# Attention scores as two 64-row products beside each other instead of one 128-row product against a key tile padded with zeros

## The chip, the cores and the metric

One core of one Trainium2 chip runs the whole program in one launch. The metric is the time of one execution in device microseconds. The kernel before took 731.09 us, the median of three runs (729.94 to 734.69).

## The reference, cut to what matters

Three stages follow each other. The attention has 8 batches, 8 heads, 576 tokens and a head width of 64; keys and values are averaged over groups of 8 tokens, which leaves 72 keys per head. A soft mixture of experts and a two-layer network come behind it.

```python
k_p = k.reshape(B, H, Sp, pool, D).mean(axis=3)            # pool 8, Sp 72
scores = scale * np.matmul(q, k_p.transpose(0, 1, 3, 2))   # (8, 8, 576, 72)
scores = scores - np.max(scores, axis=-1, keepdims=True)
attn = np.exp(scores)
attn = attn / (np.sum(attn, axis=-1, keepdims=True) + 1e-09)
attn_out = np.matmul(attn, v_p)
# then: soft mixture of experts (8 experts, 32 slots), then
h = x @ w_in; r = np.maximum(h, 0.0); g = s * (r * r) + b; out = g @ w_out
```

All of it is float32. The softmax over 72 keys is taken for each of 8 x 8 x 576 rows.

## The kernel before, in words

The first third of the program is the attention with the dispatch of its rows to the expert slots. Batches are taken in pairs (`pr` = 0 to 3), and each pair is cut into nine units of 128 token rows by some heads: unit 0 is mixed (the last 64 tokens of both batches, all heads two at a time), units 1 to 8 are pure (one batch). There are 36 units: 4 mixed and 32 pure. A pure unit takes four heads, and for each of them two token rows `t` that lie beside each other in memory: 2 x 64 numbers fill the 128 partitions of a transposed query tile.

A unit passes through six stages, named by letters, which a hand-written table (`LOOP`, `FIRST` and `TAIL`) orders so that stages of up to six units alternate on the engines' queues. Stage A (`st_A`) transposes the queries on TensorE, and ScalarE copies them into `qT` (L355). Stage B (`st_B`) makes the scores of the unit in two banks of `sc` and lets VectorE take the maximum `mx` (L390) and subtract it into `S` (L393). Stage C (`st_C`) is the exponential on ScalarE (L397), the sum and its reciprocal on VectorE (L401 to L404) and the product with it on GpSimd into `P` (L421). Stages D, E and F transpose `P` back (L434, L435), multiply it with the values that were folded with the slot matrix (L457, L464), and transpose that (L480). Between them stand the steps of `dispatch` for a finished batch (L545 to L611) and of `prep` for the next pair's keys and values (`kv_transpose`: L264 on TensorE, then copies by ScalarE, L273 for keys and L285 for values).

The pooled keys stand in `kb_t[pr % 2]`, one tile for even and one for odd pairs: 128 partitions, 16 heads of the pair, 2 x 72 columns. Partitions 0 to 63 and 64 to 127 hold the same keys, the first at columns 0 to 71 and the second at columns 72 to 143; the rest is zero, set once at the start by GpSimd (L231). So one product of 128 rows by 144 columns gives the 72 scores of both token rows (L383), four such products a unit. A mixed unit makes 16 products of 64 rows, 64 weight columns and 72 columns instead (L376), on the four quarters of the array in turn. A float32 product stands as two records in the trace, each with its own weight load, so a pure unit has eight records and a mixed one 32. Transposes by the identity have one record each.

When the attention is over, the experts' weights run over TensorE (L933, L941) while their loads still land, and the two-layer network (L1010, L1067) takes the rest.

Of the kernel before, what the change touches and what calls it, by code (L numbers as in the profile page):

```python
# [10 lines left out]
F32 = mybir.dt.float32  # L11
# [45 lines left out]
def kernel(  # L57
# [14 lines left out]
    nc = tc.nc  # L72
    B, H, SEQ, D = q.shape
    KP = SEQ // 8
# [133 lines left out]
    sc2 = sctx.enter_context(tc.tile_pool(name="sc2", bufs=2, side="right"))  # L208
    apb = bctx.enter_context(tc.tile_pool(name="apb", bufs=1, side="right"))
    P2_all = [p.tile([128, 2, H, KP], F32, name=f"P2_{i}") for i, p in enumerate((apc, apc, ap1, ap1, apb, apb))]  # L210
    pp1 = pctx.enter_context(tc.tile_pool(name="pp1", bufs=1, side="right"))
# [3 lines left out]
    def bank():  # L215
        return ps_w.tile([128, 512], F32, tag="w", name="w")
# [9 lines left out]
    make_identity(nc, ident)  # L226
    nc.vector.memset(one, 1.0)
    phi_t = pp1.tile([128, 4, 32], F32, name="phi_t")
    kb_t = [p.tile([128, 2 * H, 2 * KP], F32, name=f"kb{i}", bufs=1) for i, p in enumerate((pp1, sc2))]
    for i in range(2):  # L230
        nc.gpsimd.memset(kb_t[i], 0.0)  # L231
    for i in range(NPR):
        nc.gpsimd.memset(L_t[i], -3.0e38)

# [24 lines left out]
    def kv_transpose(nm, pr, c):  # L259

        src = kvp[nm, pr]
        ps = bank()
        for i in range(3):
            nc.tensor.transpose(  # L264
                out=ps[:, 128 * i:128 * i + 128],
                in_=src[:, 3 * c + i].rearrange("p t d -> p (t d)"),
                identity=ident,
            )
        if nm == "k":
            for h2 in range(2):  # L270
                r = slice(64 * h2, 64 * h2 + 64)
                o = kb_t[pr % 2][r, :, KP * h2 + 24 * c:KP * h2 + 24 * c + 24]
                nc.scalar.activation(  # L273
                    out=o.rearrange("p n (g u) -> p g n u", g=3),
                    in_=ps[r, 0:384].rearrange("p (g n u) -> p g n u", g=3, u=8),
                    func=ACTF.Copy, scale=1.0 / 64,
                )
            return
        if pr not in vt_t:
            vt_t[pr] = pp1.tile([128, 2, 4, KP], F32, tag="vt", name="vt", bufs=1)  # L280
        for h2 in range(2):
            r = slice(64 * h2, 64 * h2 + 64)
            o = vt_t[pr][r].rearrange("p b c x -> p (b c) x")[:, :, 24 * c:24 * c + 24]
            i_ = ps[r, 0:384].rearrange("p (g n t u) -> p g n t u", g=3, n=8, t=2)[:, :, :, h2, :]
            nc.scalar.activation(out=o.rearrange("p n (g u) -> p g n u", g=3), in_=i_, func=ACTF.Copy, scale=1.0 / 8)  # L285
# [47 lines left out]
    qT_t, S_t, P_t, P2_t, PT_t, LT_t = {}, {}, {}, {}, {}, {}  # L333
    SLOT = [5, 1, 2, 3, 4, 6, 7, 8, 9]

    def parts(jj):
        if jj == 0:
            return [(0, slice(0, 64)), (1, slice(64, 128))]
        return [(0 if jj < 5 else 1, slice(0, 128))]
# [25 lines left out]
    def st_B(t):  # L365
        pr, u = divmod(t, 9)
        qT = qT_t.pop(t)
        kb = kb_t[pr % 2]
        sc = ps_s.tile([128, 2, 512], F32, tag="sc", name="sc")
        if u == 0:  # L370

            for i in range(4):
                for x in range(2):
                    p = slice(64 * x, 64 * x + 64)
                    for bb, r in parts(0):
                        nc.tensor.matmul(  # L376
                            out=sc[r, x, KP * i:KP * i + KP], lhsT=qT[p, i, r],
                            rhs=kb[p, H * bb + 2 * i + x, KP * x:KP * x + KP], start=True, stop=True,
                        )
        else:  # L380
            bb, j = divmod(u - 1, 4)
            for i in range(4):
                nc.tensor.matmul(  # L383
                    out=sc[:, i // 2, 2 * KP * (i % 2):2 * KP * (i % 2) + 2 * KP],
                    lhsT=qT[:, i, :], rhs=kb[:, H * bb + 4 * (j % 2) + i, :], start=True, stop=True,
                )

        scv = sc[:, :, 0:288].rearrange("p x (i k) -> p x i k", k=KP)
        mx = ap2.tile([128, 2, 4], F32, tag="mx", name="mx")
        nc.vector.tensor_reduce(out=mx, in_=scv, axis=AX.X, op=ALU.max)  # L390
        S = sc2.tile([128, 2, 4, KP], F32, tag="S", name="S", bufs=2)
        S_t[t] = S
        nc.vector.tensor_tensor(out=S, in0=scv, in1=mx.unsqueeze(3).to_broadcast([128, 2, 4, KP]), op=ALU.subtract)  # L393

    def st_C(t):
        S = S_t[t]
        nc.scalar.activation(out=S, in_=S, func=ACTF.Exp)  # L397
        pr, u = divmod(t, 9)
        S = S_t.pop(t).rearrange("p x i k -> p (x i) k")
        sm = ap2.tile([128, 8], F32, tag="sm", name="sm")  # L400
        nc.vector.tensor_reduce(out=sm, in_=S, axis=AX.X, op=ALU.add)  # L401
        nc.vector.tensor_scalar(out=sm, in0=sm, scalar1=1e-9, scalar2=None, op0=ALU.add)
        rs = ap2.tile([128, 8], F32, tag="rs", name="rs")
        nc.vector.reciprocal(out=rs, in_=sm)  # L404
        rb = rs.unsqueeze(2).to_broadcast([128, 8, KP])
        if u == 0:
            P = (ap1 if pr % 2 else apb).tile([128, H, KP], F32, tag="Pm", name="Pm")
            P_t[t] = P
            o = P.rearrange("p (i x) k -> p x i k", x=2)
            S, rb = (z.rearrange("p (x i) k -> p x i k", x=2) for z in (S, rb))  # L410
        else:
            j = (u - 1) % 4
            if j % 2 == 0:
                n = 4 * pr + (u - 1) // 2
                P2 = P2_all[n % 6 if pr < NPR - 1 else n % 4]
                P2_t[0] = P2
                P_t[t], P_t[t + 1] = P2[:, 0], P2[:, 1]
            h0 = 4 * (j % 2)
            o = P2_t[0][:, :, h0:h0 + 4, :].rearrange("p t h k -> p h t k")
            S, rb = (z.rearrange("p (h t) k -> p h t k", t=2) for z in (S, rb))  # L420
        nc.gpsimd.tensor_tensor(out=o, in0=S, in1=rb, op=ALU.mult)  # L421

    def place(t):
# [196 lines left out]
    def prep(pr):  # L620


        plan_ = PLAN1 if pr == 1 else PLAN2
        plan_ = [st.split() for st in plan_.split("|")]
        eng = {op[0] + op[2]: nc.gpsimd if op[1] == "g" else nc.vector for st in plan_ for op in st if len(op) == 3}
        ch = {(nm, c): pool_chunk(nm, pr, c, eng[f"{nm}{c}"]) for nm in "kv" for c in range(3)}
        for st in plan_:
            for op in st:
                if op[0] in "kv":
                    next(ch[op[0], int(op[2])], None)  # L630
                else:
                    kv_transpose(op[0].lower(), pr, int(op[1]))
            yield
        v_prep2(pr)
        yield
        v_prep3(pr)
        yield
        v_prep1(pr)

    def first_k():  # L640
        for c in range(3):
            for _ in pool_chunk("k", 0, c, nc.vector):
                pass
        for c in range(3):
            kv_transpose("k", 0, c)
            if c == 1:
                st_A(0)

    def first_v():
        def pool_v(c, eng):  # L650
            for _ in pool_chunk("v", 0, c, eng):
                pass

        pool_v(0, nc.gpsimd)
        yield
        pool_v(1, nc.vector)
        pool_v(2, nc.gpsimd)
        yield
        kv_transpose("v", 0, 0)
        kv_transpose("v", 0, 1)  # L660
        yield
        kv_transpose("v", 0, 2)
        v_prep2(0)
        yield
        v_prep3(0)
        yield
        v_prep1(0)
# [21 lines left out]
    for t in range(NT + 2):  # L689
        for op in (FIRST.get(t) or LOOP[t % 9]).split():  # L690
            if op == "F" and t >= 7:
                st_F(t - 7)
                pr, jj = divmod(t - 7, 9)
# [60 lines left out]
    for op in TAIL.split():  # L754
        if op[0] in "FECDG":
            t = n0 + int(op[1])
# [167 lines left out]
    for n_, key in enumerate(EORD):  # L924
# [3 lines left out]
        if w_ == "w1":  # L928
            for n in range(2):
                for c in range(2):  # L930
# [3 lines left out]
                        out=l1[g][n][32 * cg:32 * cg + 32, :],  # L934
                        lhsT=siz[:, 128 * e + 32 * kc:128 * e + 32 * kc + 32],
                        rhs=w[:, c, 512 * n:512 * n + 512],
                        start=(ge == 0), stop=(ge == EG - 1),
                    )
        else:
            for c in range(4):  # L940
                nc.tensor.matmul(  # L941
                    out=so_ps[32 * c:32 * c + 32, :],
                    lhsT=h1z[:, 4 * hf + c, 36 * ge + 16 - 4 * e:36 * ge + 48 - 4 * e],
                    rhs=w[:, c, :],
                    start=(e == 0 and hf == 0), stop=(e == E - 1 and hf == 1),
# [103 lines left out]
    def part_of(blk, tt):  # L1049
        if (blk, tt) not in part_t:  # L1050
            part_t[blk, tt] = part_p.tile([128, DM], F32, name=f"part{len(part_t)}")
        return part_t[blk, tt]
# [71 lines left out]
    for i in range(len(steps)):  # L1124
# [18 lines left out]
        if t_wi:  # L1143
            f = min(t_wi)
# [5 lines left out]
        if g == len(GROUPS) - 1:  # L1150
# [8 lines left out]
            while bias:  # L1159
                p = part_of(*bias.popleft())  # L1160
# [31 lines left out]
```

## Time and profile before

| what | value |
|---|---|
| median of three runs | 731.09 us (729.94 to 734.69) |
| the profiled execution's own time | 734.33 us |
| its span, first to last instruction | 732.2 us |
| TensorE busy | 662.1 us (90% of the span) |
| VectorE busy | 501.9 us (69%) |
| ScalarE busy | 412.0 us (56%) |
| GpSimd busy | 297.1 us (41%) |
| mean granted TensorE clock | 0.960 of full speed |

The profiled execution took 3.24 us more than the median; 2.1 us of its own time lie outside the span. The attention fills about the first 228 us of the span, the experts reach to about 285 us, and the rest is the two-layer network, in which TensorE is busy nearly all the time. Engines are named PE (TensorE products), PEld (TensorE weight loads), DVE (VectorE), ACT (ScalarE), POOL (GpSimd) and SP (the queue that issues loads). A product's record reaches from its start until its result stands, so records of neighbours overlap; the distance from one start to the next tells how long TensorE was taken.

### The profile page before, as it was taken

Reading aid. Unit: us, or ns where it says so; the run is one execution under the profiler, and the core shown is the slowest. Engines: PE = TensorE matmul, PEld = TensorE weight load, DVE = VectorE, ACT = ScalarE, POOL = GpSimd, SP = SyncE. Lnnn points to the kernel's source line nnn. Section 1 sums busy time; section 2 is a strip of 40 time slices with the busy share of each in tenths; the row PEclk is TensorE's granted clock in tenths of the full one; section 3 lists DMA queues with packets and bytes.
Section 4 is the critical chain, followed back from the end, with each engine's and each line's share of the span. In section 5 each row is a group of like instructions: output and inputs, shape, how many; then the busy total and the mean of one; then the engine's idle time right before and its main releaser. Section 6 shows DMA issues by size and latency. Waiting matters only on the chain.

```text
span 732.2 us, 11203 instructions
## 1 busy us (share of the span) xinstructions
PE 662.1 (90%) x4294; PEld 517.9 (71%) x4294; DVE 501.9 (69%) x806; ACT 412.0 (56%) x713; POOL 297.1 (41%) x221
## 2 busy tenths in 40 slices
PE   4676879788877987999999999999999999999997
PEld 3565757577653325778888887878888888888885
DVE  6869778657667268788767687889655766456543
ACT  3454656466431435778665666666666666555552
POOL 3647556533210025356322443346331433799100
PEclk9886999999997998999999999999999999999999
DMA  8996455444384993101111011031100000123322
GB/s 298 375 328 209 174 168 181 172 173 164 125 288 175 379 358 123 58 0 58 59 57 59 8 61 48 1 115 59 58 1 0 1 1 1 44 95 95 100 100 87
DMA packets 41317, 88.87 MB, mean 121 GB/s; under 512 B 6960, under 2 KB 15152, under 8 KB 41264
## 3 DMA queue, kind: packets, MB, share of 16 engines
q1 hardware_dynamic: 41264, 88.16, 34.6%
q8 instruction: 34, 0.56, 0.3%
q14 instruction: 19, 0.16, 0.1%
HBM read 78.71 MB, written 9.44 MB: 120 GB/s over the span
## 4 chain that ended last, share of the span: by engine, by line
PE 75%; DVE 15%; ACT 4%; POOL 2%; issue 2%; DMA 1%; SPq 1%; DVEq 0%; ACTq 0%; POOLq 0%
PE o L1067 52%; PE h L1010 4%; PE sc L383 2%; PE l L933 2%; DVE sm L401 2%; DVE S L393 2%; PE so_ps L941 2%; DVE mx L390 2%; PE w L572 2%; PE w L434 1%; DMA ring<-in_v_dram 1%; ACT S L397 1%; PE w L591 1%; PE w L457 1%; PE ct L892 1%
## 5 line engine op out<-in xcount | busy, mean ns | idle before, releaser
L1067 PE MATMUL o<-whi,gh 128*128 128x512 f32 x576 | 229.1, 398 | 2.5 <-DVE gh L1037 2.5
L1067 PE MATMUL o<-whi,gl 128*128 128x512 f32 x576 | 225.2, 392 | 1.0 <-DVE gl L1038 1.0
L1067 PE MATMUL o<-wlo,gh 128*128 128x512 f32 x576 | 225.2, 391 | 0.0
L1019 ACT ACTIVATE r<-h 128x768 f32<-128x768 f32 x95 | 77.3, 813 | 151.8 <-PE h L1010 148.0
L1038 DVE TENSOR_TENSOR gl<-r,gh 128x768 fp32r<-128x768 f32 (+1 forms) x97 | 114.4, 1181 | 63.3 <-ACT gh L1027 62.9
L1080 DVE SCALAR_TENSOR_TENSOR part<-o,sb_t,part 128x512 f32<-128x512 f32 x144 | 99.6, 743 | 50.4 <-PE o L1067 47.8
L1067 PEld LDWEIGHTS o<-wlo,gh 128*128 128x128 f32 x576 | 108.5, 188 | 24.0
L1067 PEld LDWEIGHTS o<-whi,gh 128*128 128x128 f32 x576 | 108.4, 188 | 23.8 <-issue 5.6
L1067 PEld LDWEIGHTS o<-whi,gl 128*128 128x128 f32 x576 | 108.6, 189 | 21.7 <-DVE gl L1038 3.1
L825 POOL TENSOR_TENSOR fr<-fr,xp 128x512 f32<-128x512 f32 x28 | 41.1, 1467 | 182.4 <-ACT fr L824 160.3
L1020 ACT ACTIVATE r<-r 128x768 f32<-128x768 f32 x95 | 80.5, 847 | 3.0
L1027 ACT CAST gh<-r 128x768 fp32r<-128x768 f32 x95 | 79.4, 836 | 2.4
L421 POOL TENSOR_TENSOR P<-S,rs 128x576 f32<-128x576 f32 x32 | 37.3, 1166 | 89.7 <-DVE rs L404 54.9
L1161 POOL TENSOR_TENSOR part<-part,wsum 128x512 f32<-128x512 f32 x36 | 53.3, 1518 | 10.5 <-ACT wsum L1155 10.5
L1010 PE MATMUL h<-cT,S 128*128 128x384 f32 x192 | 48.8, 336 | 0.5 <-DVE S L853 0.5
L826 POOL TENSOR_TENSOR th<-th,fr 128x512 f32<-128x512 f32 x28 | 43.0, 1537 | 2.2
L383 PE MATMUL sc<-kb,qT 128*128 128x144 f32 x256 | 42.0, 313 | 0.0
L1010 PEld LDWEIGHTS h<-cT,S 128*128 128x128 f32 x192 | 35.9, 188 | 8.1 <-DVE S L853 0.7
L401 DVE TENSOR_REDUCE sm<-S 128x8 f32<-128x576 f32 x36 | 27.0, 750 | 21.2 <-ACT S L397 21.0
L390 DVE TENSOR_REDUCE mx<-sc 128x8 f32<-128x576 f32 x36 | 26.4, 732 | 18.7 <-PE sc L383 15.3
L383 PEld LDWEIGHTS sc<-kb,qT 128*128 128x128 f32 x256 | 37.8, 212 | 0.4 <-ACT qT L355 0.2
L397 ACT ACTIVATE S<-S 128x576 f32<-128x576 f32 x36 | 24.6, 682 | 22.1 <-DVE S L393 22.0
(212 smaller groups left out, 913.1 us busy)
## 6 DMA issues: line engine op xcount, KB each, us to landing
ring<-in_moe_w_dram SPq DMA_DIRECT2D x14, 1024.0 KB, 7.3
x<-in_moe_w_dram SPq DMA_DIRECT2D x13, 1024.0 KB, 10.5
raw<-in_moe_w_in_dram SPq DMA_DIRECT2D x8, 1024.0 KB, 5.5
raw<-in_moe_w_out_dram SPq DMA_DIRECT2D x8, 1024.0 KB, 4.8
out_dram<-part SPq DMA_DIRECT2D x32, 256.0 KB, 2.5
ring<-in_q_dram SPq DMA_DIRECT2D x7, 1024.0 KB, 9.5
ring<-in_v_dram SPq DMA_DIRECT2D x9, 768.0 KB, 10.0
ring<-in_k_dram SPq DMA_DIRECT2D x7, 768.0 KB, 7.0
```

The costliest lines, as they stand in the source:

```text
L383: nc.tensor.matmul(out=sc[:, i // 2, 2 * KP * (i % 2):2 * KP * (i % 2) + 2 * KP], lhsT=qT[:, i, :], rhs=kb[:, H * bb + 4 * (j % 2) + i, :] ...
L401: nc.vector.tensor_reduce(out=sm, in_=S, axis=AX.X, op=ALU.add)
L825: nc.gpsimd.tensor_tensor(out=fr, in0=fr, in1=xp, op=ALU.mult)
L826: nc.gpsimd.tensor_tensor(out=th if dst is None else dst, in0=th, in1=fr, op=ALU.add)
L1010: nc.tensor.matmul(out=h[x][:, 0:384] if i == 0 else h[:, x, 0:384], lhsT=Sw_t[f], rhs=cT(c, 384), start=True, stop=True)
L1019: nc.scalar.activation(out=r, in_=h[:, :, 0:384], func=ACTF.Relu)
L1020: nc.scalar.activation(out=r, in_=r, func=ACTF.Square)
L1027: nc.scalar.copy(out=gh_t[i], in_=r)
L1038: nc.vector.tensor_tensor(out=gl[:, x], in0=r[:, x], in1=gh[:, x].bitcast(F32), op=ALU.subtract)
L1067: nc.tensor.matmul(out=o_t[tt], lhsT=l[:, x, 128 * c:128 * c + 128], rhs=r, start=(fi == 0 and n == 0), stop=(fi == GROUPS[g] - 1 and n == 2),
L1080: nc.vector.scalar_tensor_tensor(out=p, in0=o_t[tt], scalar=sb_t[:, 0:1], in1=p, op0=ALU.mult, op1=ALU.add)
L1161: nc.gpsimd.tensor_tensor(out=p, in0=p, in1=wsum, op=ALU.add)
```

## The change

A pure unit's four products of 128 rows by 144 columns become eight of 64 rows by 72 columns: for each of its four heads one with partitions 0 to 63 and one with partitions 64 to 127, into the two banks of `sc`. The key tile loses its zeros and half its width, and GpSimd's two memsets of it go. The scores of a unit lie in another order, token row before head, so the view through which GpSimd writes `P` is turned accordingly. Nothing else moves.

```diff
-    kb_t = [p.tile([128, 2 * H, 2 * KP], F32, name=f"kb{i}", bufs=1) for i, p in enumerate((pp1, sc2))]
-    for i in range(2):
-        nc.gpsimd.memset(kb_t[i], 0.0)
+    kb_t = [p.tile([128, 2 * H, KP], F32, name=f"kb{i}", bufs=1) for i, p in enumerate((pp1, sc2))]
...
-                o = kb_t[pr % 2][r, :, KP * h2 + 24 * c:KP * h2 + 24 * c + 24]
+                o = kb_t[pr % 2][r, :, 24 * c:24 * c + 24]
...
-                            rhs=kb[p, H * bb + 2 * i + x, KP * x:KP * x + KP], start=True, stop=True,
+                            rhs=kb[p, H * bb + 2 * i + x, :], start=True, stop=True,
...
             for i in range(4):
-                nc.tensor.matmul(
-                    out=sc[:, i // 2, 2 * KP * (i % 2):2 * KP * (i % 2) + 2 * KP],
-                    lhsT=qT[:, i, :], rhs=kb[:, H * bb + 4 * (j % 2) + i, :], start=True, stop=True,
-                )
+                for x in range(2):
+                    p = slice(64 * x, 64 * x + 64)
+                    nc.tensor.matmul(
+                        out=sc[:, x, KP * i:KP * i + KP],
+                        lhsT=qT[p, i, :], rhs=kb[p, H * bb + 4 * (j % 2) + i, :], start=True, stop=True,
+                    )
...
-            o = P2_t[0][:, :, h0:h0 + 4, :].rearrange("p t h k -> p h t k")
-            S, rb = (z.rearrange("p (h t) k -> p h t k", t=2) for z in (S, rb))
+            o = P2_t[0][:, :, h0:h0 + 4, :]
+            S, rb = (z.rearrange("p (t h) k -> p t h k", t=2) for z in (S, rb))
```

The order of instructions on TensorE around two pure units of the second pair, before (a row is a line, the operation, out<-in, the shape of the output and how many follow each other):

```order
L435 MATMUL w<-ident,P_4_106 64x128
L591 MATMUL w<-sel_62,at 72x32 x8
L383 MATMUL sc<-kb_124,qT 128x144 x4
L353 MATMUL w<-ident,ring_84 128x128 x4
L601 MATMUL w<-a,vps 128x64 x4
```

The same place after the change; line numbers shift by up to two:

```order
L436 MATMUL w<-ident,P_4_106 64x128
L592 MATMUL w<-sel_62,at 72x32 x8
L384 MATMUL sc<-kb_124,qT 128x72 x8
L351 MATMUL w<-ident,ring_84 128x128 x4
L602 MATMUL w<-a,vps 128x64 x4
```

The products of the pure unit stand at the same place of the queue, eight for four, each half as wide; their neighbours are the same. It is so at all 32 pure units.

On GpSimd, at the start of the program, before:

```order
L231 MEMSET kb_123 128x2304
L231 MEMSET kb_124 128x2304
L233 MEMSET L_72 128x352
...
L246 TENSOR_TENSOR ring_83<-ring_83 128x3x256
L250 TENSOR_TENSOR ring_83<-ring_83 128x3x128
L251 TENSOR_TENSOR vp<-ring_83 128x384
...
L421 TENSOR_TENSOR Pm<-S,rs 128x2x4x72
L421 TENSOR_TENSOR P_0_102<-S,rs 128x4x2x72 x2
```

And after the change:

```order
L231 MEMSET L_72 128x352
...
L244 TENSOR_TENSOR ring_83<-ring_83 128x3x256
L248 TENSOR_TENSOR ring_83<-ring_83 128x3x128
L249 TENSOR_TENSOR vp<-ring_83 128x384
...
L422 TENSOR_TENSOR Pm<-S,rs 128x2x4x72
L422 TENSOR_TENSOR P_0_102<-S,rs 128x2x288 x2
```

The two memsets of `kb` are gone, and the products that write `P` of pure units (not `Pm`, that of the mixed ones) write two runs of 288 numbers instead of eight of 72. The other engines' queues hold the same rows in the same order.

## Rows read from the trace of the kernel before

**Rows 1.** The page: busy time of each engine, its share of the span, instructions.
```profile
PE 662.1 (90%) x4294; PEld 517.9 (71%) x4294; DVE 501.9 (69%) x806; ACT 412.0 (56%) x713; POOL 297.1 (41%) x221
```
**Rows 2.** Stretches: us; busy PE, PEld, DVE, ACT, POOL; granted clock, DMA, GB/s.
```profile
43.00:81.00 38.00, 25.64 (x263) 20.30 (x261) 33.54 (x52) 20.57 (x48) 23.98 (x19) 0.82 0.70 247
81.00:130.00 49.00, 41.36 (x490) 33.64 (x490) 37.37 (x74) 31.14 (x78) 27.61 (x23) 0.97 0.51 171
...
290.00:732.00 442.00, 436.54 (x2043) 358.06 (x2041) 299.47 (x407) 274.20 (x371) 180.13 (x120) 1.00 0.14 48
```
**Rows 3.** The chain of work, 17 to 228 us: its lines' shares.
```profile
by line: PE sc L383 8.6%; DVE sm L401 6.6%; DVE S L393 6.5%; DVE mx L390 5.8%; PE w L572 5.3%; PE w L434 5.0%; DMA ring<-in_v_dram 4.8%; ACT S L397 3.8%; issue 3.0%; PE w L591 2.9%; PE w L457 2.9%; PE w L601 2.7%; DVE dd L554 2.5%; PE w L35
```
**Rows 4.** The chain's pieces at pure units: start us, us, what; followers too.
```profile
29.10 1.92 PE sc L383 x8
31.02 0.66 PE w L264 x3
...
160.03 1.06 PE sc L383 x8
161.10 0.63 PE w L307 x32
...
201.04 1.08 PE sc L383 x8
202.12 0.02 issue
```
**Rows 5.** Timeline of PE around a pure unit: start us, us, instruction.
```profile
57.03 0.27 PE L435 MATMUL w<-ident,P 128*64 128x128 f32 x1
57.14 1.15 PE L383 MATMUL sc<-kb,qT 128*128 128x144 f32 x8
58.12 0.49 PE L264 MATMUL w<-ident,vp 128*128 128x128 f32 x3
```
**Rows 6.** Timeline of PE around a mixed unit.
```profile
59.54 0.27 PE L435 MATMUL w<-ident,P 128*64 128x128 f32 x1
59.74 0.73 PE L376 MATMUL sc<-kb,qT 64*64 64x72 f32 x32
60.40 0.66 PE L353 MATMUL w<-ident,ring 128*128 128x128 f32 x4
```
**Rows 7.** Timeline of PE around a transpose that loads 64 rows.
```profile
120.67 0.60 PE L353 MATMUL w<-ident,ring 128*128 128x128 f32 x4
121.21 0.52 PE L326 MATMUL w<-ident,vpt 64*128 64x64 f32 x5
121.65 0.55 PE L264 MATMUL w<-ident,kp 128*128 128x128 f32 x3
```
**Rows 8.** Records by line: ns shortest/median/longest; then weight loads of L601 in time.
```profile
L383 PEld LDWEIGHTS sc<-kb,qT x256: 187/190/338, 17.4 to 201.7; 128*128 128x128 f32 x128
L376 PE MATMUL sc<-kb,qT x128: 222/223/379, 13.6 to 164.4; 64*64 64x72 f32 x128
...
112.22 0.97 PEld L601 LDWEIGHTS w<-a,vps 72*128 72x128 f32 x8
```
**Rows 9.** Timeline of PE around a pure unit at the lower clock.
```profile
69.25 2.12 PE L383 MATMUL sc<-kb,qT 128*128 128x144 f32 x8
```
**Rows 10.** Groups by line: busy us, mean ns, idle before and its releasers.
```profile
L383 PE MATMUL sc<-kb,qT 128*128 128x144 f32 x256 | 42.0, 313 | 0.0
...
L390 DVE TENSOR_REDUCE mx<-sc 128x8 f32<-128x576 f32 x36 | 26.4, 732 | 18.7 <-PE sc L383 15.3 <-PE sc L376 3.3
...
L246 POOL TENSOR_TENSOR ring<-ring 128x768 f32<-128x768 f32 x10 | 18.4, 1843 | 10.9 <-DMA ring<-in_v_dram 10.9
```
**Rows 11.** GpSimd's lines: ns shortest/median/longest, first and last start.
```profile
L231 POOL MEMSET kb<- x2: 2017/2018/2018, 1.2 to 3.2; 128x2304 f32 x2
...
L421 POOL TENSOR_TENSOR P<-S,rs x32: 1147/1149/1687, 28.2 to 206.4; 128x576 f32<-128x576 f32 x32
...
L421 POOL TENSOR_TENSOR Pm<-S,rs x4: 1147/1150/1152, 26.6 to 169.3; 128x576 f32<-128x576 f32 x4
```

## Prediction

> **What bounds the kernel now.** I read the page first. TensorE is busy 90% of the span and VectorE 69% [rows 1], but that mixes stages: from 290 us on TensorE works 436.5 of 442 us, while in the attention it works 25.6 of 38 us in one stretch and 41.4 of 49 in another [rows 2]. The change touches the attention alone, so only its wait structure counts. The chain of waits from 17 to 228 us (211 us) changes hands between two engines: of the lines that its listing names, TensorE's six sum to 27.4% and VectorE's four to 21.4% [rows 3]. Its largest single line is the score product of pure units, L383, with 8.6%, or 18 us, of the 42.0 us that this line is busy in all [rows 10]: 43% of its work lies on the chain. It does so 14 times in 32 units (the first and the last of the 14 stand in [rows 4]). After eight of these pieces the chain stays on TensorE at a transpose or a sum, after one it goes to L307, after five to VectorE's maximum.
>
> The timeline then shows how a unit stands in the queue. TensorE comes straight from the block before (L435 starts at 57.03, L383 at 57.14) and goes straight on at 58.12 [rows 5]: 0.98 us for eight records, 0.12 each. The idle time before L383 is 0.0 us [rows 10]. What is added to or taken from a unit therefore moves all that stands behind it in TensorE's queue: mostly the next query transposes (then ScalarE's `qT` and the next unit), else L264 or the sum L563.
>
> **The products.** Eight records of 144 columns become eight pairs of 72 columns, the two of a pair on the two halves of the array's rows. The columns that one half takes are the same half, 0.06 us a record. Four prices decide.
>
> *Do the two of a pair run beside each other?* The mixed unit has 32 records on four quarters. They take 0.73 us with the last record's 0.22 us in it [rows 6, 8], so 0.51 us for 31 starts, 0.016 each or 0.066 per round of four. That is hardly over the 0.06 us of one such record, so quarters, rows against rows too, load and multiply together. I take pairs as concurrent.
>
> *How fast do pairs follow each other?* Each half must load 128 columns of weights a record, whatever its rows. The nearest row is L601, also 128 weight columns, with 64 to multiply: eight loads in 0.97 us, the last 0.19 long, so (0.97 - 0.19) / 7 = 0.111 us a load [rows 8]. There the load sets the step. Now the product does, at 0.12. The lower bound is the mixed unit's 0.066, with 64 weight columns. I take 0.111, since the count of weight columns is the same.
>
> *What do the borders cost?* From L435 to a pure unit's first record it is 0.11 us [rows 5], to a mixed unit's first 0.20 [rows 6], and to L326, which loads 64 rows by 128 columns and so has just the new form, 121.21 less the last of four L353 starts (120.67 + 0.60 - 0.27 = 121.00), again 0.21 [rows 7]. So entering costs 0.09 us more, and the first weights are loaded in the open instead of behind the block before: 0.11. Leaving: the mixed unit's last record starts at 59.74 + 0.73 - 0.22 = 60.25, the next block at 60.40, so 0.15, of which 0.06 is the product; and that block's four transposes last 0.66 us instead of 0.60 [rows 6, 7], 0.06 for their open first load. The Trainium skill, "TensorEngine Tiling (Array Packing)", Key Properties, says that changing the tiling mode drains the engine while another tile of the same mode does not. By that rule the two borders pay and the eight changes between halves do not; these rows agree (0.09 us at a border, 0.016 between quarters).
>
> *Sum of a unit.* 0.09 + 8 x 0.111 + 0.15 + 0.06 = 1.19 us, for 0.98 before: **+0.21 us**. At the lower clock (1.2 GHz) a unit takes 1.92 us [rows 4], so I double it: +0.42. Five units run so: 27 x 1.15 + 5 x 2.12 is 41.7 of the line's 42.0 us [rows 5, 9, 10]. The scores are ready for VectorE later by less: before, the last record starts 0.86 us after the first and lasts 0.29; now 0.09 + 0.89 = 0.98 us after that same moment, and lasts 0.22. That is 1.20 for 1.15, **+0.05 us**.
>
> On the chain: eight pieces that go on on TensorE, three of them at the lower clock, 5 x 0.21 + 3 x 0.42 = 2.3 us; L307 is a 64-row form itself and pays its border already, so 0.21 - 0.09 - 0.06 = +0.06; five that go to VectorE, one at the lower clock, 4 x 0.05 + 0.10 = 0.3. Together **+2.7 us**. If all 32 units counted in full it would be 27 x 0.21 + 5 x 0.42 = 7.8 us. Beside the 18 other units VectorE, GpSimd or a transfer ends last and has slack, but not without limit; I add a quarter of the 5.1 us between, 1.3: **+4.0 us**. The shift reaches the end whole, since the experts' products start on the last result of the attention.
>
> **The rest, at nothing.** The two memsets of 2.02 us lie at 1.2 to 5.2 us [rows 11], and GpSimd then waits 10.9 us for the first values' transfer [rows 10]; the copies into the tile have to wait for the first keys' transfer too. GpSimd's product into `P` takes 1149 ns in eight runs of 72 and 1150 ns in the other order of the mixed units [rows 11], so the form of its output does not show; two runs of 288 have no row, and I take 0. ScalarE's copies into the key tile and VectorE's reads of the scores keep their counts. No transfer moves.
>
> The profiled execution took 734.3 us, so the sum gives 738.3 in its terms. It lies 3.2 us above the median; against the median of 731.1 I forecast **735.1 us**. 1% is 7.3 us (the three runs lie 4.75 us apart): within 1% is 723.8 to 738.4.
>
> **Rivals.**
>
> *The clock falls more often: slower.* Where TensorE was busy 67% of a stretch its mean clock was 0.82, at 84% it was 0.97, at 99% 1.00 [rows 2]. The change makes a unit's columns stream for 8 x 0.06 = 0.48 us instead of 0.98, with open loads and borders between; the attention may spend more time at 1.2 GHz. A mean lower by 0.05 is a tenth more of the 211 us at half speed: 21 us, three quarters busy, 8 us of added TensorE time, 43% of it on the chain, 3.4. With my 4.0 that is 738.5; at 0.10 lower it is 742. From 0.05 on it passes the 1% line. Against it: while TensorE waits in borders its records still stand, and longer blocks fill gaps. Price 740; chance 0.20.
>
> *A half's load waits for its own product: slower.* The Trainium skill, "TensorE: Matmul & The Clock Gate", Part 3, says that a weight load overlaps products in flight only when its row group differs. That would give steps of 0.111 + 0.06 = 0.171 us and units of 1.61, +0.63 (scores +0.47): 5 x 0.63 + 3 x 1.26 + 0.48 + 6 x 0.47 = +10 us, 741. The trace speaks against the mechanism: loads of L383 on all rows take 0.11, products 0.12, and both fit into 0.98 us eight times [rows 5, 8]; rounds of the mixed unit follow at 0.066. Chance 0.04.
>
> *Half the rows load faster: faster.* If pairs step at the mixed unit's 0.066 us, a unit is 0.09 + 0.11 + 7 x 0.066 + 0.15 + 0.06 = 0.87, -0.11, and the scores come 0.27 earlier. On the chain: -5 x 0.11 - 3 x 0.22 - 0.26 - 6 x 0.27 = -3 us, 728. It turns to a gain from a step under 0.081. For it: 72 columns could be fed that fast. Against it: L601's step with 128 weight columns. Chance 0.09, of which 0.03 goes to a full halving. The Trainium skill's tiling page, Theoretical Speedup, promises up to twofold at 64 rows. Twofold without borders would be -0.49 a unit, and with the four slow pieces counted twice 18 x 0.49 = -9 us, 722; the borders of [rows 6, 7] speak against it.
>
> *Nothing.* VectorE bounds the units and hides the rest: 731. Against it: eight chain pieces that stay on TensorE. Chance 0.07.
>
> My forecast has 0.60; its own range is +2.7 to +7.8, 733.8 to 738.9. The range of 8 in 10 leaves out the twofold case, some of the faster one and the slow cases beyond 743: 728.5 to 743. Faster by over 1%: the twofold case and little else, 0.04. Slower by over 1%: most of the clock's 0.20, the 0.04, and the upper end of my own range, 0.07: 0.30. Within: 0.66.
>
> **What would show it.** In the new profile a pure unit should stand as 16 records with the form 64*128, 0.2 us after the start of the record before, its loads stepping by 0.11 us a pair, and the next block's start about 1.2 us after where L383's first record would have stood. The line's share of the chain should not fall. A step near 0.066 or 0.17 decides for one of the two rivals on loads; a mean clock from 17 to 228 us that is lower by 0.05 or more, for the clock. I am wrong if units got longer as said and the attention still ended no later: then the slack beside them was larger than the chain shows.

## The result, and the profile after

The changed kernel takes 742.75 us, median of four runs (738.10, 742.60, 742.90, 743.51), against 730.67 for the kernel before: ratio 1.0136, interval 1.0100 to 1.0172. That is slower by 10 to 12 us, well over the 735.1 forecast, on the far side of the 1% line, and a quarter of a microsecond inside the range that ended at 743. The profiled execution is the fastest of the four, 738.10 us with a span of 735.8 and a mean clock of 0.954; of the other three, spans and clocks alone stand: 742.60 us with 0.954, 743.51 with 0.945, 742.90 with 0.933. So a comparison of the two profiles, 738.1 with 734.3, shows a third of the loss. Medians below are over all runs; ratios and mean clocks leave out runs over 1.5% above the fastest of their kernel (two of e1's six, one each of e2's and e9's).

The page: busy time of the engines, to be read beside [rows 1].

```profile
PE 673.4 (92%) x4550; PEld 520.4 (71%) x4550; DVE 498.1 (68%) x806; ACT 412.4 (56%) x713; POOL 293.3 (40%) x219
```

TensorE is busy for 11.3 us more, ScalarE does what it did, and GpSimd has lost 3.8 us, the two memsets. VectorE has lost 3.8 us too, by a copy at the start that ran beside the memsets (e1, which keeps them, has it at 4.38 us again). Before, and then after:

```profile
2.26 4.37 DVE L238 COPY selrep<-sel 128x128 f32<-128x128 f32 x1 [0.55 <-ACT selrep L236]
```

```profile
2.26 0.45 DVE L236 COPY selrep<-sel 128x128 f32<-128x128 f32 x1 [0.55 <-ACT selrep L234]
```

The timeline of TensorE and then of its weight loads at the unit of [rows 5], with the block before and behind:

```profile
60.26 0.27 PE L436 MATMUL w<-ident,P 128*64 128x128 f32 x1
60.46 1.12 PE L384 MATMUL sc<-kb,qT 64*128 64x72 f32 x16
61.51 0.55 PE L262 MATMUL w<-ident,vp 128*128 128x128 f32 x3
...
60.46 0.97 PEld L384 LDWEIGHTS sc<-kb,qT 64*128 64x128 f32 x16 [0.20 <-issue]
```

From the start of the block before to that of the block behind it is 61.51 - 60.26 = 1.25 us, before 58.12 - 57.03 = 1.09, and the three transposes behind last 0.55 us for 0.49. Together +0.22 us, for +0.21 forecast. The entry takes 0.20 us. The sixteen loads take 0.97, of which the last is 0.19 long and starts some 0.01 after its partner: (0.97 - 0.20) / 7 = 0.110 us a pair, for 0.111.

A unit at the lower clock, to be read beside [rows 9]:

```profile
72.24 0.42 PE L436 MATMUL w<-ident,P 128*64 128x128 f32 x1
72.59 1.99 PE L384 MATMUL sc<-kb,qT 64*128 64x72 f32 x16
74.50 0.90 PE L351 MATMUL w<-ident,ring 128*128 128x128 f32 x3
```

The same unit in the kernel before, the blocks around the row of [rows 9]:

```profile
69.03 0.42 PE L435 MATMUL w<-ident,P 128*64 128x128 f32 x1
...
71.17 0.84 PE L353 MATMUL w<-ident,ring 128*128 128x128 f32 x3
```

From start to start 74.50 - 72.24 = 2.26 us, before 71.17 - 69.03 = 2.14, and 0.06 for the three transposes behind: +0.18 in all, where I had doubled the 0.21.

The chain from 17 to 228 us, beside [rows 3], and the records of the line:

```profile
by line: PE sc L384 8.3%; DVE S L394 6.5%; DVE sm L402 5.9%; DVE mx L391 5.8%; PE w L573 5.6%; DMA ring<-in_v_dram 5.2%; PE w L435 5.1%; PE w L458 3.6%; PE w L351 3.3%; ACT S L398 3.2%; issue 3.1%; PE w L592 2.9%; PE w L262 2.1%; DVE dd L55
...
L384 PE MATMUL sc<-kb,qT x512: 271/272/486, 18.6 to 203.1; 64*128 64x72 f32 x171
```

The score line's share of the chain has not risen; it fell from 8.6%, where I had said that it should not fall. Longer units do not show as a longer stay on the chain. What did change is the clock of the first stretches. The stretches of the attention (busy us of PE, PEld, DVE, ACT, POOL; then the granted clock, the share of the DMA engines, GB/s), first the three of the kernel before that do not stand above:

```profile
17.00:43.00 26.00, 19.13 (x166) 16.84 (x165) 16.95 (x29) 12.48 (x30) 15.15 (x11) 0.80 1.06 371
...
130.00:180.00 50.00, 41.33 (x513) 33.27 (x513) 33.73 (x75) 28.07 (x71) 19.48 (x16) 0.93 0.42 150
180.00:230.00 50.00, 37.80 (x414) 29.69 (x416) 32.30 (x85) 17.72 (x47) 7.88 (x7) 0.87 0.64 225
```

And the changed kernel, where [rows 2] have 0.82 and 0.97 in its second and third stretch:

```profile
17.00:43.00 26.00, 21.75 (x180) 17.64 (x179) 16.24 (x26) 10.45 (x25) 15.15 (x11) 0.74 1.06 361
43.00:81.00 38.00, 29.02 (x311) 22.73 (x310) 31.92 (x54) 20.89 (x48) 22.16 (x18) 0.77 0.66 216
81.00:130.00 49.00, 41.37 (x545) 32.11 (x545) 37.16 (x73) 29.93 (x75) 27.01 (x23) 0.97 0.52 175
130.00:180.00 50.00, 43.74 (x571) 33.38 (x569) 33.61 (x75) 30.44 (x75) 20.84 (x18) 0.93 0.42 152
```

Up to 81 us the clock is lower, and TensorE is busier (21.75 for 19.13, 29.02 for 25.64) with VectorE doing less (16.24 for 16.95, 31.92 for 33.54). VectorE's maximum of the sixth unit and that of the 35th, first in the kernel before and then in the changed one:

```profile
44.48 0.71 DVE L390 TENSOR_REDUCE mx<-sc 128x8 f32<-128x576 f32 x1
...
195.14 0.75 DVE L390 TENSOR_REDUCE mx<-sc 128x8 f32<-128x576 f32 x1
```

```profile
47.66 0.71 DVE L391 TENSOR_REDUCE mx<-sc 128x8 f32<-128x576 f32 x1
...
197.96 0.75 DVE L391 TENSOR_REDUCE mx<-sc 128x8 f32<-128x576 f32 x1
```

The sixth unit is 3.2 us late, the 35th 2.8. Between them the changed kernel loses nothing, though TensorE is busy for longer. The same 150 us of work, 3 us later in the changed kernel:

```profile
48.00:198.00 150.00, 119.54 (x1397) 96.85 (x1397) 113.94 (x223) 85.39 (x209) 72.55 (x59) 0.92 0.52 179
```

```profile
51.00:201.00 150.00, 124.08 (x1609) 95.86 (x1610) 113.38 (x224) 86.24 (x211) 72.73 (x60) 0.92 0.53 178
```

TensorE works 4.5 us more there at the same mean clock, 0.92, and VectorE gets as much done. From 17 to 228 us as a whole the clock is 0.88 for 0.89, so this pair of profiles does not show the fall by 0.05 that I had named as the sign of the clock:

```profile
17.00:228.00 211.00, 163.63 (x1828) 133.30 (x1826) 151.99 (x307) 109.53 (x268) 94.09 (x76) 0.89 0.62 217
```

```profile
17.00:228.00 211.00, 174.28 (x2081) 135.02 (x2079) 149.04 (x300) 110.21 (x268) 94.19 (x76) 0.88 0.63 217
```

The chain's piece in which the experts' products begin, of the kernel before and then of the changed one:

```profile
228.37 9.08 PE l L933 x56
```

```profile
232.18 8.01 PE l L934 x45
```

It begins 3.8 us later, which is the 3.6 us of the span. The profiles speak for the clock, but they hold a third of the loss, so runs have to tell whether the longer units or the clock did the rest.

### The profile page after: what moved, and what is told of

Its sections match the earlier page's. It is cut to its first block, busy times and chain, and to the rows that moved or that the text cites. A ratio compares the mean times of both kernels' runs of the same rounds, so it can differ in the third digit from the quotient of the medians.

```text
span 735.8 us, 11711 instructions
## 1 busy us (share of the span) xinstructions
PE 673.4 (92%) x4550; PEld 520.4 (71%) x4550; DVE 498.1 (68%) x806; ACT 412.4 (56%) x713; POOL 293.3 (40%) x219
## 4 chain that ended last, share of the span: by engine, by line
PE 75%; DVE 15%; ACT 3%; POOL 2%; issue 2%; DMA 1%; SPq 1%; DVEq 0%; ACTq 0%; POOLq 0%
PE o L1068 51%; PE h L1011 4%; PE l L934 2%; PE sc L384 2%; DVE S L394 2%; DVE sm L402 2%; DVE mx L391 2%; PE so_ps L942 2%; PE w L573 2%; DMA ring<-in_v_dram 1%; PE w L435 1%; PE w L458 1%; PE w L351 1%; ACT S L398 1%; PE ct L893 1%
## 5 line engine op out<-in xcount | busy, mean ns | idle before, releaser
L384 PE MATMUL sc<-kb,qT 64*128 64x72 f32 x512 | 40.8, 306 | 0.0
L384 PEld LDWEIGHTS sc<-kb,qT 64*128 64x128 f32 x512 | 35.9, 213 | 6.0 <-issue 5.1
L353 ACT COPY qT<-w 128x512 f32<-128x512 f32 x36 | 21.1, 586 | 31.1 <-PE w L351 30.6
```

The source lines that it names most:

```text
L384: nc.tensor.matmul(out=sc[:, x, KP * i:KP * i + KP], lhsT=qT[p, i, :], rhs=kb[p, H * bb + 4 * (j % 2) + i, :], start=True, stop=True,)
```

## The experiments

Theory U: the added TensorE time of a unit is the loss. Theory C: with the shorter products TensorE's clock falls more often, and that is the loss. The first four runs set them against each other, by adding and shortening work on TensorE.

**e1, the products alone.** The key tile keeps its zeros and its memsets.

```diff
-    kb_t = [p.tile([128, 2 * H, KP], F32, ...
+    kb_t = [p.tile([128, 2 * H, 2 * KP], F32, ...
+    for i in range(2):
+        nc.gpsimd.memset(kb_t[i], 0.0)
...
-                        lhsT=qT[p, i, :], rhs=kb[p, H * bb + 4 * (j % 2) + i, :], ...
+                        lhsT=qT[p, i, :], rhs=kb[p, H * bb + 4 * (j % 2) + i, KP * x:KP * x + KP], ...
```

Expected: 

> The pure units' eight 64-row products and the turned order of P stay, but the key tile keeps its zeros, its width and GpSimd's two memsets. Theory U (the added TensorE time of a unit, +0.21 us, is the loss) and theory C (columns that stream for half as long let the clock fall more often, and that is the loss) both expect the changed kernel's ratio again, 1.010 to 1.017. A third, that the memsets or the narrower tile matter, expects 1.00 to 1.005 here.

Measured: median 744.55 us, ratio 1.0115 (1.0068 to 1.0161), as the changed kernel. The memsets and the narrower tile are worth nothing that shows. The turned order of `P`, which e1 keeps, costs GpSimd nothing either: 1149 ns in the changed kernel as in [rows 11]. So the products are the change. The profile of e1 also holds a warning about the clock. Its second stretch, a unit in it, and the row of `P` in the changed kernel:

```profile
17.00:43.00 26.00, 21.74 (x178) 17.62 (x177) 16.32 (x26) 10.53 (x25) 15.15 (x11) 1.00 1.07 367
...
38.47 1.99 PE L386 MATMUL sc<-kb,qT 64*128 64x72 f32 x16
```

```profile
L422 POOL TENSOR_TENSOR P<-S,rs x32: 1147/1149/1687, 29.3 to 207.7; 128x576 f32<-128x576 f32 x32
```

The granted clock stands there as 1.00, but the unit takes 1.99 us, as at the lower clock in the changed kernel. So the record of the clock can leave out a lower clock at the start of a run, and the mean of this one (0.961) is too high.

**e2, the quarters.** Each 64-row product is cut into two of 64 weight columns.

```diff
+                    for r in (slice(0, 64), slice(64, 128)):
                         nc.tensor.matmul(
-                            out=sc[:, x, KP * i:KP * i + KP], lhsT=qT[p, i, :], ...
+                            out=sc[r, x, KP * i:KP * i + KP], lhsT=qT[p, i, r], ...
```

Expected: 

> Each 64-row product is cut into two of 64 weight columns, on the four quarters of the array, as the mixed units have them. By the mixed unit's rows a unit then takes 0.20 + 0.51 + 0.15 + 0.165 = 1.03 us from the last start before it to the second of the next block, for 1.20 in the kernel before and 1.41 in the changed one. Theory U: shorter units, so faster than before by 2 to 6 us (0.992 to 0.998). Theory C: columns stream as briefly as in the changed kernel, so slower than before all the same, by 3 to 9 us, with a mean clock as low as there.

Measured: 741.64 us, ratio 1.0116 (1.0073 to 1.0158), mean clock 0.941 (0.962 for the kernel before). The unit did get shorter. In the timeline of this kernel, in an execution of 746.44 us, it reads

```profile
49.43 0.38 PE L482 MATMUL w<-ident,LT 128*128 128x128 f32 x2
49.74 0.73 PE L385 MATMUL sc<-kb,qT 64*64 64x72 f32 x32
50.40 0.66 PE L436 MATMUL w<-ident,P 128*128 128x128 f32 x4
```

0.66 us for the 0.98 of [rows 5], so with the borders 0.2 us less than before. And the kernel is as slow as the changed one. Its stretches:

```profile
81.00:130.00 49.00, 39.80 (x645) 29.89 (x646) 34.88 (x70) 28.74 (x71) 24.70 (x21) 0.86 0.48 154
130.00:180.00 50.00, 44.36 (x676) 33.98 (x675) 32.69 (x71) 28.56 (x70) 20.82 (x18) 0.80 0.40 143
180.00:230.00 50.00, 41.81 (x548) 31.34 (x547) 29.55 (x69) 19.67 (x50) 9.51 (x9) 0.73 0.59 207
```

0.86, 0.80 and 0.73 where the kernel before has 0.97, 0.93 and 0.87. TensorE is busier in the last two (44.36 for 41.33, 41.81 for 37.80) with shorter units, because what it does takes up to twice as long in more of the time (1.92 us for 0.98 in [rows 4] and [rows 5]). Theory U has no room for this.

**e3 and e4, one product more.** The kernel before, and the changed one, with a product of the identity ahead of each pure unit's query transposes, which overwrite it.

```diff
+        for _ in range(1 if u else 0):
+            nc.tensor.matmul(out=ps[:, 0:128], lhsT=ident, rhs=ident, start=True, stop=True)
         for i in range(4):
             nc.tensor.transpose(out=ps[:, 128 * i:128 * i + 128], in_=src[i], identity=ident)
```

Expected of e3: 

> The kernel before, with one product of the identity with itself (two records, 0.218 us at the full clock) ahead of each pure unit's query transposes, into a place that they then overwrite: TensorE time of +0.21 us a unit as in the changed kernel, but on all rows, without a border and with its columns streaming. Theory U: as slow as the changed kernel, +4 to +12 us. Theory C: +0 to +4 us, with the clock no lower than before.

Expected of e4: 

> The changed kernel with the same product of the identity ahead of each pure unit's query transposes. Theory U: slower than the changed kernel by 4 to 12 us, 1.019 to 1.03 against the kernel before. Theory C: the streaming comes back, the clock with it, and the kernel is as slow as the changed one or less, 1.005 to 1.015.

Measured: e3 731.62 us, ratio 0.9991 (0.9965 to 1.0018), mean clock 0.967; e4 739.80 us, 1.0091 (1.0064 to 1.0117), mean clock 0.957. In the kernel before the same +0.21 us a unit costs nothing on balance: its clock rose from 0.962 to 0.967, so part of the price may have come back that way. In the changed kernel it does not add to the loss, and there too the clock is higher, 0.957 for 0.947.

**e5 to e8, the waits filled.** Products of the identity stand in fifteen waits of TensorE, ahead of the instruction that waits, so that the clock is held and the units are compared at nearly the same clock.

```diff
+    FILL = {"D0": 10, "k12": 8, "k20": 5, "v31": 8, "m0": 18, "m2": 3, "m4": 2, "m6": 4, "c3": 4,
+            "z1": 9, "z2": 7, "z4": 3, "z5": 8, "z6": 3, "p7": 10}
+    def fill(key, ps):
+        for _ in range(FILL.get(key, 0)):
+            nc.tensor.matmul(out=ps[:, 0:128], lhsT=ident, rhs=ident, start=True, stop=True)
...
         ps = bank()
+        fill(f"z{b_}", ps)
         nc.tensor.matmul(out=ps[:, 0:32], lhsT=one.to_broadcast([128, 128]), rhs=zd, start=True, stop=True)
```

Expected of e5: 

> The kernel before, with products of the identity with itself (102 in all, 0.214 us each at the full clock) at fifteen places where TensorE waits for over 1 us in its trace, into places that are overwritten next. Each group is shorter than the wait that it fills. Theory C: the clock falls less often, mean 0.975 to 0.99 over the span, and the kernel is faster than before by 3 to 8 us. Theory U: no change, since the waits end when they did; at most 1 us.

Expected of e6: 

> The changed kernel with the same products in the waits. Theory C: with the clock held, what is left between this one and the kernel before with filled waits is the unit's added TensorE time, 2 to 5 us (by the chain's 2.7 to 4.0), and the clocks of the two lie within 0.008 of each other. Theory U: the difference stays at 9 to 12 us.

Expected of e7: 

> The quarters (64 rows by 64 weight columns) with the same products in the waits. Theory C: their shorter units now show: 1 to 5 us faster than the kernel before with filled waits, and 4 to 11 us faster than the kernel before, 0.985 to 0.995. If the quarters have another cost than the clock (the borders, twice the instructions), they stay slower than the kernel before with filled waits.

Expected of e8: 

> The kernel before with filled waits and the one product of the identity ahead of each pure unit's query transposes: +0.214 us of TensorE time a unit with the clock held. By the chain's share, 43% of 7 us, it is slower than the kernel before with filled waits by 2 to 5 us; if TensorE's time had no price there, by under 1 us.

| run | what | median us | ratio to before | mean clock |
|---|---|---|---|---|
| e5 | before, filled | 728.33 | 0.9933 (0.9907 to 0.9959) | 0.985 |
| e6 | changed, filled | 728.11 | 0.9937 (0.9916 to 0.9958) | 0.982 |
| e7 | quarters, filled | 726.77 | 0.9913 (0.9885 to 0.9940) | 0.980 |
| e8 | before, filled, one product more a unit | 728.97 | 0.9947 (0.9925 to 0.9970) | 0.985 |

The kernel before gets 5 us faster by 102 products that no result needs. The changed one gets some 14 us faster by the same, and nothing that shows is left between the two. That is less than the 2 to 5 us that I expected of theory C: even the unit's price falls away. e8 gives that price by itself at an unchanged clock, 728.97 against 728.33, under 1 us for 7 us of added TensorE time; the scatter of the runs leaves room for 2. The quarters, slower than the kernel before without fillings, come out ahead of all by about 1.5 us, which their interval doesn't set apart from e5. So their form has no price of its own that shows. The stretches of e6:

```profile
43.00:81.00 38.00, 31.15 (x360) 24.87 (x360) 33.69 (x52) 20.43 (x48) 23.97 (x19) 0.96 0.74 253
81.00:130.00 49.00, 45.69 (x597) 36.87 (x597) 37.40 (x74) 31.32 (x78) 27.61 (x23) 1.00 0.53 178
130.00:180.00 50.00, 48.36 (x670) 39.19 (x670) 35.42 (x79) 29.80 (x76) 20.36 (x17) 1.00 0.46 164
180.00:230.00 50.00, 44.80 (x505) 32.30 (x501) 36.36 (x97) 17.56 (x47) 8.07 (x8) 0.97 0.61 221
```

0.96, 1.00, 1.00, 0.97, and VectorE does more in each stretch than in the changed kernel (33.69 for 31.92 up to 81 us): the work comes earlier. Its chain from 17 to 228 us:

```profile
by line: DVE S L402 8.3%; DVE sm L410 7.6%; DVE mx L399 7.3%; PE sc L392 6.9%; DMA ring<-in_v_dram 4.2%; PE w L585 4.2%; ACT S L406 3.7%; PE w L444 3.1%; PE w L223 3.0%; PE w L604 2.9%; issue 2.8%; PE l L947 2.7%; DVE raw L251 2.6%; PE w L3
```

VectorE's three lines of the softmax now lead, and TensorE's score line has fallen to 6.9%. That fits a unit's 0.21 us having no price there.

**e9, streaming given back to the quarters.** The edit of e3, made in e2.

Expected: 

> The quarters, waits not filled, with the one product of the identity ahead of each pure unit's query transposes: a unit takes 1.03 + 0.22 = 1.25 us, about as long as in the kernel before (1.20), but 0.21 us more of it streams than in the quarters. Theory C: more work and less time, faster than the quarters (1.0116 of before) by 3 to 8 us, with a mean clock over 0.95. A price of TensorE's time alone: slower than the quarters by 1 to 5 us.

Measured: 737.58 us, ratio 1.0049 (1.0018 to 1.0080), mean clock 0.955. More work and 4 us less time than the quarters, as theory C has it. It also says that a unit as long as before (1.25 us) is not enough: the clock and the time stay between those of the quarters and of the kernel before.

**e10, the longest waits of e7 filled further.**

```diff
-    FILL = {"D0": 10, "k12": 8, ... "m0": 18, ... "p7": 10}
+    FILL = {"D0": 16, "D3": 4, "k12": 12, ... "m0": 25, ... "p7": 16}
```

Expected: 

> The quarters with filled waits, the five longest that are left filled further (29 more products of the identity). Theory C: the clock up to 43 us rises from 0.74, and the time falls by 0 to 2 us more, 0.988 to 0.992 of before. If the fillings are now longer than the waits, it is slower than the quarters with filled waits by up to 3 us.

The fillings added are 27 products, not the 29 that I wrote. Measured: 727.19 us, ratio 0.9926 (0.9899 to 0.9952), mean clock 0.983. In the profiles the clock between 17 and 43 us did rise, from 0.74 to 0.87, but the time shows no gain over e7.

## Why the prediction was right in direction and wrong in its likeliest case

- **Pairs run beside each other, a pair steps by 0.111 us, borders cost 0.09 us and open loads.** Right: 0.110 us a pair, 0.20 at the entry, +0.22 for a unit at the full clock. The rival in which a half's load waits for its own product is out (0.171 a pair), and so is the one in which half the rows load faster (0.066). The rule of the Trainium skill, "TensorE: Matmul & The Clock Gate", Part 3, on loads that overlap only across row groups, does not hold here. The twofold speed of the Trainium skill, "TensorEngine Tiling (Array Packing)", Theoretical Speedup, did not come either. With 128 weight columns a pair steps by 0.110 us; with 64, in e2, the 32 records take the 0.73 us of the mixed unit, 0.066 a round. And my rows agreed less with the rule on drains than I said: L435 stands in the form 128*64 and L383 in 128*128, with 0.11 us between their starts [rows 5], so this change of form pays no border.
- **The lower clock doubles it, +0.42.** Wrong: +0.18. None of my rows showed a border at the lower clock.
- **The sum on the path, +4.0 us.** This step failed. I took the chain's share of the line, 43%, as the price of added time. In the profiles 29 units in a row, each longer but for the mixed ones, add nothing to the 3.2 us that the changed kernel was late by then, at the same clock. e8 measured +0.6 us for 7 us of added time, e6 against e5 -0.2, and e3 -0.4 with a clock that rose. A share of a chain tells who ended last, not how much slack stands beside it; with filled waits VectorE's softmax leads the chain. So the direction did not come out right by this sum, and that the two profiles lie 3.8 us apart, close to my 4.0, is luck: their loss arose before the sixth unit and behind the 35th.
- **The clock falls more often (given 0.20).** This was the case. The quarters are shorter and lose as much, at a mean clock of 0.941; with filled waits the changed kernel and the one before are equal, at 0.982 and 0.985. I priced it at 738.5 for a mean lower by 0.05 in the attention and 742 for 0.10, of which 4.0 us are the sum's and 3.4 and 6.8 the clock's. The changed kernel's four runs have a mean of 0.947 over the span, 0.962 before: if all of the fall lies in the attention, 0.0155 of 735 us is 0.054 of its 211. The mean of the four times is 741.8, so the fall was the one I named; but with the 4.0 near nothing, 3.4 us stand for some 10. The error is the same share of 43%, used again. What a given fall costs is not settled. A line through the 23 runs of the kernel before gives 6.4 us for 0.01 of mean clock, but these scatter (730.0 to 735.1 us at 0.963 alone); e5 against the kernel before gives about 2 (4.8 us for 0.022), e7 against e2 nearly 4 (14.9 for 0.039). By these 0.0155 is worth 10, 3 or 6 us. And the changed kernel's two runs with 0.954 took 738.10 and 742.60, so the mean over the span does not fix the time, be it that it matters where the clock falls or that the record has gaps as in e1. At the lower clock all of TensorE's work in a stretch takes up to twice as long at once, and the slack that hides 0.21 us here and there need not hide that.
- **The rest at nothing.** Right, by e1.

What stays open: which part of the shorter units lets the clock fall, the shorter products themselves or the open loads and borders around them, since no run has the one without the other; and how much of the 10 to 12 us each fall of the clock costs, since no run of the changed kernel over 738.10 us left a trace.

## What to carry to other kernels

Where TensorE waits often, its clock is part of the price of every edit: look up the granted clock by stretch first, and expect that shorter products can lower it (from 0.962 to 0.941 with the quarters). Useless work in its waits, put into both kernels, tests this in two runs and separates the clock from the edit; here it gained 5 us on the kernel before, and the edit gained nothing. Follow one instruction of each unit through both profiles: where the lag grows is where the time is lost. Do not price added work by its share of the chain unless the next engine's slack is known.

## What the runs showed of the hardware

102 useless products in waits made the kernel 0.7% faster, with the mean clock up from 0.963 to 0.985 (e5). The Trainium skill, "TensorE: Matmul & The Clock Gate", Why this matters for your kernels, advises against idle gaps of TensorE amid a kernel. e5 agrees. Two products on the two halves of the rows start some 0.01 us apart and load their 128 weight columns side by side, 0.110 us a pair, where one product with 128 weight columns takes 0.111 [rows 8]. A VectorE copy beside GpSimd's memsets took 4.37 us, without them 0.45. And one core's kernel has no fixed clock from run to run: the kernel before spans 0.958 to 0.967 in 23 runs, 728.8 to 737.1 us.
